# A list scheduler's planned landing times corrected by a table per kind and batch, with a new set of priorities, in a fused attention and MLP kernel

## The chip, the cores and the metric

The kernel runs on one core of one Trainium2 chip. The metric is the device time of one execution in microseconds (us), as the median of three runs. The core has a matrix engine (TensorE, here PE), a vector engine (VectorE, DVE), a scalar engine (ScalarE, ACT), GpSimd (POOL) and SyncE (SP). They run their own instruction streams, each in the order in which it was built, and wait for one another by semaphores. In this kernel POOL issues the loads, and SP issues the transposing transfers and the stores.

## The reference

Masked attention with two kinds of mask, and then a two-layer MLP over all tokens (8 batches of 576 tokens, 8 heads of 64):

```python
B, H, S, D = 8, 8, 576, 64          # x becomes 4608 x 512
scores = scale * (q @ k.transpose)
mask_local = (rel >= 0) & (rel < 32)                       # heads 0 to 3
mask_strided = (rel >= 0) & (pos_k % 32 == pos_q % 32)     # heads 4 to 7
attn = softmax(where(mask, scores, -1e9))
x = (attn @ v)                       # heads side by side, 4608 x 512
h = maximum(x @ w_in, 0)             # 512 -> 2048
out = (s * h * h + b) @ w_out        # 2048 -> 512
```

## The kernel before

**Attention.** The heads of one batch b form four units (b, m): m = 0 and 1 are pairs of local heads, m = 2 and 3 pairs of strided ones. For each unit PE makes the scores (line 840, into the banks ps_s, from kT_loc, kT_alt or a transposed strided key and from the queries spread in qD_loc and qD_str); ACT takes the exponential (858, p_loc, p_str); DVE or POOL apply the mask (866); PE multiplies by the values (901, v_loc, v_str, into ps_a or ps_t); DVE takes the reciprocal of the row sums (918) and multiplies (928, x_nat), which frees the PE bank; x_nat is transposed to xT, by PE (948) or by a DMA (978, and 970 with 974 by way of DRAM). From batch 3 or 4 on, queries and keys are transposed by DMA too: q_dma (788 local, qTl; 796 strided, qT2) and k_dma (768 local, kT_loc and kT_alt; 779 strided, whose place is called vs0 or vs1 after the buffer it reuses, so "vs<-ks" is a key). Copies on DVE or ACT spread qTl and qT2 into qD_loc and qD_str (603).

**MLP.** Tokens go in nine blocks T of 512. The first GEMM (1308, 1549) reads xT and w_in, ACT applies the relu (1330), squares follow (1337, 1339, 1489); the result is gT. The second GEMM (1164, 1276) uses seven products in place of eight (Strassen's scheme) with sums of gT (1043) and of w_out (w_mix, w_sum). A product that completes a quarter of the output is combined on DVE into a tile o (1089), of which there are three, and stored from SP (1111). A fourth combine waits until the first tile's store has landed.

**What sets the order.** All of this is put in order at build time by the class Plan, a list scheduler with a clock of its own. PE's steps are taken one by one; whenever a step is emitted, `flush` places the work of the other engines (a Post) whose needs are met in its clock, the one with the smallest ready time plus priority first. Posts of kind D, X and Y are DMAs of SP: transposes (planned latency 12 us), stores to DRAM and transposes back. `land` gives the planned landing of loads from POOL. The priorities are nine dictionaries ORDER, one for each stretch of the plan's clock (26, 60, 110, 135, 160, 185, 215 and 250 us), with a number for each kind of work ("c11" is the combine of the fourth quarter, "qT" the transposes of queries, "x@V" a bias for x_nat on DVE). The planned times do not run on the chip: they decide only which instruction stands where, and a wrong one makes an engine wait for something behind which other work is queued. `keep_running` lets PE do small filler matmuls (1825, 1830) where the plan has no step.

## Time and profile before

| | |
|---|---|
| median of three runs | 295.19 us (294.97 to 295.9) |
| profiled execution | 295.52 us, its span 293.7 us |
| PE busy | 286.4 us (98%), at the full clock (1.00) |
| DVE / ACT / POOL busy | 232.7 / 207.0 / 97.2 us |
| matmuls | 2873 |

The page's busy times are those of one execution. The chain of waits follows the work that ended last back to its start; a row of a table of waits names the waiting engine and line and, behind the arrow, what ended the wait. In rows of the profile buffer numbers are left out: ps_a stands for ps_a0. Times are counted from the start of the span.

### The profile page before, as it was taken

To read this page: it belongs to the slowest core of one execution; us is meant where nothing else is said; L and a number is where in the kernel's file an instruction comes from. 1 tells how busy PE (TensorE), PEld (TensorE's weight loads), DVE (VectorE), ACT (ScalarE), POOL (GpSimd) and SP (SyncE) were. 2 spreads that over 40 slices of the span, in tenths; PEclk is the share of its full clock that TensorE was granted. 3 is DMA by queue.
4 is the path that set the end of the run, shared out by engine and by line. 5 is a ranking of instruction groups with operands and counts; after the bars stand their busy time and mean duration, and the time that the engine had idled before them with its cause. 6 is when DMAs were issued, how large, how long until landed. Compare 5 with 4: busy or idle time off the path is not lost.

```text
span 293.7 us, 7265 instructions
## 1 busy us (share of the span) xinstructions
PE 286.4 (98%) x2873; PEld 227.2 (77%) x2873; DVE 232.7 (79%) x515; ACT 207.0 (70%) x352; POOL 97.2 (33%) x150
## 2 busy tenths in 40 slices
PE   7999999999999999899999999999999999999995
PEld 3774655666676778799867876799899999999984
DVE  5763887999998699769734998499999877787954
ACT  3559855999998893569789855788756685576700
POOL 8983623610941690339220970540000000000010
PEclk9999999999999999999999999999999999999999
DMA  8999999999999799989997999964212210310214
GB/s 130 193 206 203 214 182 179 192 190 144 132 141 185 80 116 166 138 191 149 202 185 109 128 166 156 161 131 143 57 42 78 71 38 0 109 36 3 72 37 144
DMA packets 95720, 38.18 MB, mean 130 GB/s; under 512 B 73318, under 2 KB 94054, under 8 KB 95686
## 3 DMA queue, kind: packets, MB, share of 16 engines
q0 software_dynamic: 49904, 18.22, 61.3%
q1 hardware_dynamic: 45782, 19.51, 34.6%
q8 instruction: 22, 0.36, 0.5%
q14 instruction: 12, 0.10, 0.1%
HBM read 36.99 MB, written 10.62 MB: 162 GB/s over the span
## 4 chain that ended last, share of the span: by engine, by line
PE 49%; issue 32%; DVE 8%; DMA 4%; POOL 3%; ACT 2%; POOLq 0%; DVEq 0%
PE ps_f L1308 21%; PE ps_f L1164 11%; DMA out_dram<-o 4%; PE ps_s L840 3%; PE ps_f L1580 3%; PE ps_a L901 2%; DVE x_nat L928 1%; PE ps_s L1580 1%; PE ps_t L948 1%; PE ps_f L715 1%; DVE p_loc L866 1%; PE ps_t L715 1%; PE ps_t L901 1%; DVE v_str L603 1%; DVE gT L1339 1%
## 5 line engine op out<-in xcount | busy, mean ns | idle before, releaser
L1308 PE MATMUL ps_f<-xT,w_in_sb 128*128 128x512 f16 (+2 forms) x472 | 100.2, 336 | 0.0
L1330 ACT ACTIVATE gT<-ps_f 128x512 f16<-128x512 f32 x91 | 53.7, 599 | 24.1 <-PE ps_f L1308 19.4
L1164 PEld LDWEIGHTS <-gT 128*128 128x128 f16 x640 | 61.0, 98 | 10.8
L1308 PEld LDWEIGHTS <-w_in_sb 128*128 128x128 f16 x480 | 47.5, 114 | 17.5 <-issue 0.2
L1164 PE MATMUL ps_f<-w_out_sb,gT 128*128 128x256 f16 x400 | 58.2, 273 | 0.0
L1337 ACT ACTIVATE gT<-gT 128x1024 f16<-128x1024 f16 x32 | 33.7, 1062 | 0.7
L1218 POOL TENSOR_TENSOR qD_str<-cp_u,kT_loc 128x512 f32<-128x512 f32 x1 | 1.3, 1262 | 89.3 <-issue 89.3
L1489 ACT ACTIVATE gT<-gT 128x1024 f16<-128x1024 f16 x24 | 25.4, 1058 | 5.3 <-DVE gT L1471 4.2
L1164 PE MATMUL ps_f<-w_mix,gT 128*128 128x256 f16 x208 | 28.9, 273 | 0.0
L1043 DVE TENSOR_TENSOR gT<-gT 128x1024 f16<-128x1024 f16 x40 | 27.2, 698 | 0.2
L928 DVE TENSOR_TENSOR x_nat<-ps_a,rec 96x384 f16<-96x384 f32 (+2 forms) x48 | 24.7, 515 | 0.6
L858 ACT ACTIVATE p_loc<-ps_s 128x384 f16<-128x384 f32 x46 | 20.6, 497 | 3.5 <-PE ps_s L840 3.2
L858 ACT ACTIVATE p_str<-ps_s 72x432 f16<-72x432 f32 (+1 forms) x46 | 20.6, 482 | 2.7 <-PE ps_s L840 2.4
L581 POOL DMA_DIRECT2D v_loc<-in_v_dram x24 | 17.8, 759 | 9.7 <-DMA w_out_sb<-in_moe_w_out_dram 5.9
L1549 PEld LDWEIGHTS <-w_in_sb 128*128 128x128 f16 x176 | 19.3, 114 | 0.5
L901 PEld LDWEIGHTS <-p_str 72*128 72x128 f16 x256 | 13.4, 97 | 5.2 <-issue 1.6
L1164 PE MATMUL ps_f<-w_mix,S 128*128 128x256 f16 x112 | 16.6, 273 | 0.0
L1089 DVE SCALAR_TENSOR_TENSOR o<-ps_f,sb_all,cp_v 128x512 f32<-128x512 f32 x14 | 10.4, 744 | 7.8 <-PE ps_f L1164 5.8
L1043 DVE TENSOR_TENSOR S<-gT 128x1024 f16<-128x1024 f16 x20 | 13.7, 684 | 3.2 <-PE ps_f L1164 3.1
L918 DVE RECIPROCAL rec<-ps_a 96x6 f32<-96x6 f32 (+2 forms) x48 | 8.7, 182 | 9.4 <-PE ps_a L901 9.1
L603 POOL COPY v_str<-v_str 72x512 f16<-72x512 f16 x10 | 6.3, 654 | 28.2 <-DMA v_str<-in_v_dram 28.1
L1580 PE MATMUL ps_f<-w_out_sb,gT 128*128 128x512 f16 x48 | 14.0, 380 | 0.0
(275 smaller groups left out, 589.4 us busy)
## 6 DMA issues: line engine op xcount, KB each, us to landing
out_dram<-o SPq DMA_DIRECT2D x34, 256.0 KB
w_in_sb<-in_moe_w_in_dram POOLq DMA_DIRECT2D x4, 512.0 KB, 9.5
w_out_sb<-in_moe_w_out_dram POOLq DMA_DIRECT2D x4, 512.0 KB, 9.9
qs<-in_q_dram POOLq DMA_DIRECT2D x6, 288.0 KB, 7.9
ks<-in_k_dram POOLq DMA_DIRECT2D x6, 288.0 KB, 9.1
v_loc<-in_v_dram POOLq DMA_DIRECT2D x24, 72.0 KB, 9.8
ql<-in_q_dram POOLq DMA_DIRECT2D x4, 288.0 KB, 9.4
kl<-in_k_dram POOLq DMA_DIRECT2D x16, 72.0 KB, 3.9
```

The source lines that it names most:

```text
L581: nc.gpsimd.dma_start(out=vl[LPAD:128, h, :, 0:D], in_=v_band(b, h))
L858: nc.scalar.activation(out=st["pw", g][0:nk, 0:2 * n * nq], in_=st["s", g][0:nk, 0:2 * n * nq], func=AF.Exp, scale=scale)
L901: nc.tensor.matmul(out=st["pa", g][:, n % 6, :], lhsT=st["pw", gp_][0:nk, i * nq:i * nq + WIDE], rhs=vt[0:nk, 2 * mm + e, j, :])
L928: nc.vector.tensor_tensor(out=x_at(0, cnt), in0=st["pa", g][0:nq, 0:cnt, 0:D], in1=st["rec", g][0:nq, 0:cnt].to_broadcast([nq, cnt, D]), o ...
L1043: {"V": nc.vector, "P": nc.gpsimd}[eng].tensor_tensor(out=at(out), in0=at(x), in1=at(y), op=op)
L1164: nc.tensor.matmul(out=gts[name, T][:, t], lhsT=lhs(k, t), rhs=rhs(k), start=fresh and t == k == 0, stop=t == 1 and k == H - 1, skip_group ...
L1308: nc.tensor.matmul(out=gts["h", T, ft][:, lo:hi], lhsT=w_in_sb[ft // 4][:, ct].rearrange("p (x l) -> p l x", l=4)[:, ft % 4], rhs=xT[ct][: ...
L1330: nc.scalar.activation(out=u, in_=gts["h", T, ft], func=AF.Relu)
L1337: nc.scalar.activation(out=g, in_=g, func=AF.Square)
L1489: nc.scalar.activation(out=g_, in_=g_, func=AF.Square)
L1549: nc.tensor.matmul(out=st[bk][:, 256 * t + lo:256 * t + hi], lhsT=lhs(t, c), rhs=x, start=fresh and t == c == lo == 0, stop=t == c == 1 an ...
L1580: nc.tensor.matmul(out=gts[id_], lhsT=gts[T][:, ft, ts * 128:(ts + 1) * 128], rhs=w_out_sb[:, ft, cols], start=(ft == 0), stop=(ft == NFT ...
```

## The change

A table MORE of 57 numbers (in nanoseconds, between -9000 and +6500) holds corrections of the planned landing times, per kind of load or transfer and batch, and the method `more` looks them up. `land` adds them to loads, `flush` to the transfers of kinds D, X and Y. All nine dictionaries of ORDER have new numbers. No operation, tile or buffer is changed: PE's real matmuls are as many and of the same sizes on every line, and the fillers of line 1830 are 32 in place of 28. Lines behind the table are numbered 36 higher after the change (L1089 is now L1125).

```diff
@@ class Plan
+    @staticmethod
+    def more(k, eng="P"):
+        if k[0] == "in":
+            name, b = k[1], k[2]
+        elif k[0] == "raw":
+            name, b = ("vs", k[3]) if k[1] == "v" else (k[1] + "l" * (len(k[1]) == 1), k[2])
+        elif k[0] in ("k", "qT"):
+            name, b = "T" + k[0][0] + "ls"[k[1][1] // 2], k[1][0]
+        elif k[0] == "xT":
+            name, b = "Txl" if eng == "D" else "Txi", k[1]
+        elif k[0] == "xd":
+            name, b = "Txo", k[1][0]
+        elif k[0] == "soon":
+            name, b = k[0], k[1][0]
+        else:
+            return 0.0
+        return MORE.get(name + str(b), 0.0)
+
     def land(self, keys, cost, late=0.0):
+        late += self.more(keys[0])
...
-                self.done[k] = end + over + ((9000.0 if k[1][0] >= 5 else 6000.0) if soon else p.lat or self.LAT[eng])
+                self.done[k] = end + over + (
+                    (9000.0 if k[1][0] >= 5 else 6000.0) if soon else p.lat or self.LAT[eng]) + (
+                    self.more(k, eng) if eng in "DXY" else 0.0)
...
+MORE = {"Tkl4": 1000.0, "Tkl5": -3500.0, "Tkl7": -1000.0, "Tks3": -5500.0, "Tks4": 1000.0,
+        "Tks5": -6000.0, "Tks6": -9000.0, "Tks7": -9000.0, "Tql6": -6000.0, "Tql7": 2000.0,
...
-    {"SLACK": 1000.0, "ahead": 0.52, "lead": 0.4, "q0": -1500.0, "q": -1160.0, "q@A": -770.0,
...
```

(T stands for a transfer from SP: Tkl the transposes of local keys, Tks of strided ones, Tql and Tqs of queries; the digit is the batch.)

How the rows of the engines move is shown at three places. The first is DVE at 74 to 79 us of the profile, batch 2: the multiplication x_nat, the mask of p_loc and the copies that put values into v_loc1 and v_str1. Before:

```order
L928 TENSOR_TENSOR x_nat_1317<-ps_a0_157,rec_1329 72x384
L603 COPY v_loc1_96<-v_loc1_96 32x2x5x64
L603 COPY v_str1_98<-vs0_105 72x8x64 x4
L603 COPY v_loc1_96<-v_loc1_96 32x2x5x64
L918 RECIPROCAL rec_1380<-ps_a0_157 72x6
L866 TENSOR_TENSOR p_loc0_111<-p_loc0_111,masks_83 128x1152
L928 TENSOR_TENSOR x_nat_1317<-ps_a0_157,rec_1380 72x384
```

After:

```order
L964 TENSOR_TENSOR x_nat_1320<-ps_a0_157,rec_1341 72x384
L902 TENSOR_TENSOR p_loc0_111<-p_loc0_111,masks_83 128x1152
L639 COPY v_loc1_96<-v_loc1_96 32x2x5x64
L954 RECIPROCAL rec_1370<-ps_a0_157 72x6
L639 COPY v_str1_98<-vs0_105 72x8x64 x2
L964 TENSOR_TENSOR x_nat_1320<-ps_a0_157,rec_1370 72x384
L639 COPY v_loc1_96<-v_loc1_96 32x2x5x64
L639 COPY v_str1_98<-vs0_105 72x8x64 x2
```

The second x_nat of the unit stood behind both v_loc copies, all four v_str copies and the mask; it now stands behind the mask, one v_loc copy and two v_str copies, and the other copies follow it.

The second place is DVE at 118 to 123 us, where the second GEMM of block T = 2 begins to give output. o_2038 (before) and o_2044 (after) are the combine that takes over the first o tile of its three, after the store of o_1902 or o_1874; x_nat rows on ps_a0 and ps_t0 free those banks. Before:

```order
L1043 TENSOR_TENSOR gT_1462<-gT_1462 128x4x256 x2
L1089 SCALAR_TENSOR_TENSOR cp_v_115<-ps_f21_161,sb_all_85,bcs_91 128x512
L1043 TENSOR_TENSOR gT_1462<-gT_1462 128x4x256 x2
L918 RECIPROCAL rec_2030<-ps_a0_157 72x4
L1089 SCALAR_TENSOR_TENSOR o_2038<-ps_f20_160,sb_all_85,cp_v_115 128x512
L918 RECIPROCAL rec_2052<-ps_t0_154 72x6
L928 TENSOR_TENSOR x_nat_1896<-ps_a0_157,rec_2030 72x256
L928 TENSOR_TENSOR x_nat_2033<-ps_t0_154,rec_2052 72x384
```

After:

```order
L954 RECIPROCAL rec_2007<-ps_t0_154 72x4
L954 RECIPROCAL rec_2011<-ps_a0_157 72x6
L1125 SCALAR_TENSOR_TENSOR cp_v_115<-ps_f20_160,sb_all_85,bcs_91 128x512
L1079 TENSOR_TENSOR gT_1460<-gT_1460 128x4x256 x2
L964 TENSOR_TENSOR x_nat_2000<-ps_a0_157,rec_2011 72x384
L1125 SCALAR_TENSOR_TENSOR o_2044<-ps_f21_161,sb_all_85,cp_v_115 128x512
L964 TENSOR_TENSOR x_nat_1935<-ps_t0_154,rec_2007 72x256
```

Before, both x_nat (ps_a0, ps_t0) stand behind the combine; after, the one on ps_a0 stands ahead of it and the one on ps_t0 behind. Between o_1902 and o_2038 stood 15 rows with 17 instructions; between o_1874 and o_2044 stand 19 with 20. o_1902 stood behind an x_nat and S (the sum of gT) that follow o_1874 now.

The third place is SP at 102 to 128 us: the stores of block T = 1 (out), the transposes of batch 4's x (xT0, xT1) and those of batch 5's queries (qTl, qT2) and keys (kT_alt, vs0). Before:

```order
L788 DMA_TRANSPOSE qTl_1883<-ql_1712 128x6x96 x2
L1111 DMA out_0_dram<-o_1902 128x2x256
L978 DMA_TRANSPOSE xT0_107<-x_nat_1839 128x6x96
L978 DMA_TRANSPOSE xT1_108<-x_nat_1805 128x6x96
L1111 DMA out_0_dram<-o_1921 128x2x256
L1111 DMA out_0_dram<-o_1950 128x2x256
L768 DMA_TRANSPOSE kT_alt_1958<-kl_1717 128x6x96
L768 DMA_TRANSPOSE kT_alt_1961<-kl_1717 128x6x96
L796 DMA_TRANSPOSE qT2_1988<-qs_769 128x8x80 x2
L779 DMA_TRANSPOSE vs0_105<-ks1_118 128x8x80 x2
```

After:

```order
L1147 DMA out_0_dram<-o_1874 128x2x256
L824 DMA_TRANSPOSE qTl_1892<-ql_1725 128x6x96 x2
L804 DMA_TRANSPOSE kT_alt_1901<-kl_1730 128x6x96
L804 DMA_TRANSPOSE kT_alt_1904<-kl_1730 128x6x96
L1014 DMA_TRANSPOSE xT1_108<-x_nat_1829 128x6x96
L1014 DMA_TRANSPOSE xT0_107<-x_nat_1758 128x6x96
L1147 DMA out_0_dram<-o_1931 128x2x256
L1147 DMA out_0_dram<-o_1973 128x2x256
L832 DMA_TRANSPOSE qT2_1994<-qs_772 128x8x80 x2
L815 DMA_TRANSPOSE vs0_105<-ks1_118 128x8x80 x2
```

The first store passes the two qTl transposes, and the two kT_alt transposes pass xT and two stores; qT2, vs0 and the last store stay where they were. PE's order around this place moves too: from the step of line 901 that waits for the x_nat above (six matmuls on ps_a0 before, four on ps_t0 after) to the first matmul on kT_alt stood 55 matmuls and stand 28; from there to the first on vs0 stood 58 and stand 46.

At the head of the program (17 to 21 us), the last pieces of x_nat of the first batch's two strided units (72x256) move from DVE to ACT, where each is four activations of 72x64, ahead of the copies to xT2 and xT3. On DVE there are 461 rows after and 473 before, on ACT 344 and 331, on POOL 93 and 95, on SP 81 and 77.

## The prediction, made before the run

> **What bounds the kernel now.** I read the busy times of the page first, then the stretches of the span, then what the matrix engine waits for, and last the chain of waits.

> ```profile
> span 293.7 us, 7265 instructions
> PE 286.4 (98%) x2873; PEld 227.2 (77%) x2873; DVE 232.7 (79%) x515; ACT 207.0 (70%) x352; POOL 97.2 (33%) x150
> ...
> 110.00:135.00 25.00, 24.25 (x257) 21.42 (x256) 20.42 (x45) 14.08 (x26) 7.92 (x14) 1.00 1.43 158
> 135.00:160.00 25.00, 25.00 (x226) 19.23 (x225) 15.31 (x33) 22.02 (x34) 8.37 (x13) 1.00 1.37 170
> ```

> The matrix engine, PE, is busy in 286.4 of 293.7 us. In a row of a stretch the first number after its length is PE's busy time, and the two numbers before the last are the granted clock (1.00) and the share of the 16 DMA engines, which is over 1 because packets overlap. From 135 us on PE has no idle time that the profile shows, and its real matmuls are the same in number and size after the change (only fillers differ). So the change can win no more than PE's idle time, and that is listed:

> ```profile
> PE ps_a L901 <- DVE x_nat L928: 1.1, 2, 0.7
> PE ps_s L1825 <- PEq L1928: 0.8, 1, 0.8
> PE ps_t L707 <- DMA ql<-in_q_dram: 0.6, 1, 0.6
> PE ps_f L901 <- POOL v_loc L603: 0.5, 1, 0.5
> PE ps_t L948 <- DVE x_nat L928: 0.4, 1, 0.4
> PE ps_a L707 <- DMA kl<-in_k_dram: 0.2, 1, 0.2
> PE ps_f L840 <- DVE kTs L603: 0.2, 1, 0.2
> PE ps_a L901 <- DVE p_str L866: 0.2, 1, 0.2
> ```

> Each row gives microseconds in all, how often, and the longest. They sum to 4.0 us. The PEq row is the start of the program and the ql, kl, v_loc and kTs rows belong to the first batch (0.6 + 0.2 + 0.5 + 0.2 = 1.5 us), ahead of which the change moves nothing but the size of some fillers: these 2.3 us stay. What can go is x_nat 1.1, x_nat 0.4 and p_str 0.2: **1.7 us**.

> **The head (17 to 42 us).** The 0.4 us is a transposing matmul at 19.1 us that waits for an x_nat. DVE makes three of these in a row there, while ACT waits:

> ```profile
> 18.52 1.31 DVE L928 TENSOR_TENSOR x_nat<-ps_f,rec 72x384 f16<-72x384 f32 x3
> 17.03 0.17 ACT L1639 ACTIVATE sb_all<-ps_f 128x2 f32<-128x2 f32 x1
> 19.69 0.64 ACT L603 COPY xT<-ps_t 128x576 f16<-128x576 f16 x1 [1.83 <-PE ps_t L948]
> ```

> ACT stood 1.83 us ahead of its copy at 19.69 (the bracket). The change gives two narrow pieces of x_nat (72x256) from DVE to ACT, each as four activations of 72x64. DVE is relieved of about 0.4 us each (1.31 for three), so the 0.35 to 0.4 us wait can go. No row has a 72x64 activation; the smallest near it is 0.17 (128x2), so eight take at least 1.4 us, within the 1.83 us that ACT is idle. But they stand ahead of the xT copy, and the second four need a reciprocal that DVE made about 20 us, so that the copy at 19.69 can come some 0.5 us later and the first GEMM with it. I take -0.2, with ends of -0.5 (this and the p_str wait go) and +0.5.

> **The wait at 78.9 us.** The chain of waits (start, duration, what) shows what DVE does in front of it:

> ```profile
> 76.00 1.10 DVE v_str L603 x4
> 77.14 0.41 DVE v_loc L603
> 77.67 0.76 DVE p_loc L866
> 78.42 0.48 DVE x_nat L928
> 78.94 0.28 PE ps_a L901 x4
> ```

> PE stood 0.33 us there (the smaller of the two x_nat waits of ps_a). In the new order the x_nat comes after only two of the four v_str copies and one v_loc copy: 0.55 us and 0.41 us of copies now stand behind it, 0.96 in all, which is more than 0.33. The copies are late by nothing that PE waits for soon, since the values they prepare are read later. I take -0.3; ends -0.4 and 0 (something else on DVE, the reciprocal for example, holds x_nat).

> **The wait at 122.4 us.** This is the longest one, 0.7 us, and its cause lies twelve microseconds back:

> ```profile
> 109.28 0.60 DVE S L1043
> 109.88 0.67 DVE o L1089
> 110.57 10.51 DMA out_dram<-o
> 121.17 0.75 DVE o L1089
> 122.02 0.31 DVE x_nat L928
> 122.38 0.34 PE ps_a L901 x6
> ...
> DVE o L1089 <- DMA out_dram<-o: 2.0, 1, 2.0
> ```

> The last row is from the waits of DVE. There are three o tiles. The fourth combine after 109.88 (o_2038) needs the first one's tile, whose store landed at 121.1; DVE was ready at 121.17 - 2.0 = 119.15 and stood 2.0 us. The x_nat that frees PE's bank stands behind it. PE lost 0.75, so it would have borne some 1.25 us of DVE's wait. Between the two combines DVE worked without a pause from 110.55 to 119.15, 8.6 us for 17 instructions (15 rows), 0.51 us each. In the new order 19 rows with 20 instructions stand between the same two combines: by the mean 1.5 us more, by kinds (two x_nat, a p_str, an S and a reciprocal more, two gT fewer, at some 0.5, 0.7, 0.6, 0.1 and 0.6) about 1.1. The wait shrinks to 0.5 to 0.9 us, below the 1.25 us that PE bears. The next x_nat for ps_a0 even stands ahead of the combine now, but the one for ps_t0, which PE's next step of attention wants first, still stands behind it. So the wait goes if the store takes about as long as before: -0.7, with an end at 0 (the store takes 1 us more, or the waits change banks).

> **What takes its place.** The transposes of batch 5 are issued from SP. First its timeline, then a row of its waits, then two steps of PE in the chain:

> ```profile
> 102.39 3.18 SPq L788 DMA_TRANSPOSE qTl<-ql  x2
> 110.57 0.38 SPq L1111 DMA_DIRECT2D out_dram<-o  x1
> 111.05 4.13 SPq L978 DMA_TRANSPOSE xT<-x_nat  x2
> 115.27 1.07 SPq L1111 DMA_DIRECT2D out_dram<-o  x2
> 116.50 5.62 SPq L768 DMA_TRANSPOSE kT_alt<-kl  x2
> 122.25 3.11 SPq L796 DMA_TRANSPOSE qT<-qs  x2
> 125.90 2.53 SPq L779 DMA_TRANSPOSE vs<-ks  x2
> ...
> SPq L1111 <- DVE o L1089: 4.9, 1, 4.9
> ...
> 127.82 0.33 PE ps_s L840 x4
> 132.90 0.38 PE ps_s L840 x6
> ```

> The store that DVE was late with now stands ahead of the two qTl, which had gone out 8 us before it; kT_alt goes ahead of xT; qT and vs stay last. PE's order wants batch 5 sooner: from the step at 122.38 to the first kT_alt step (127.7) stood 55 matmuls and now 28, and from there to the first step that reads vs (132.7) 58 and now 46. These 39 matmuls at (132.74 - 122.38) / 113 = 0.092 us are 3.6 us: vs is wanted at 129.1, or 128.4 when the wait at 122.4 is gone. When can it be there? The store's combine passes one x_nat and S, 0.49 + 0.60 us, so the store can be issued about 109.5. From there SP's rows add up: 0.4 + 3.2 (qTl) + 5.6 (kT_alt) + 4.1 (xT) + 1.1 (stores) + 3.1 (qT) + 2.5 (vs) = 20.0, to 129.5, against 128.4 before. The first vs, which alone is needed, is through about 1.3 us sooner, 128.2, and must land. PE wants it at 128.4. kT_alt in turn ends near 118.7 and is wanted near 124.2: covered by 5 us. xT moves 4 us later and feeds the stage at 130 and on; the two stores behind it have over 8 us until their tiles come round. So the new wait is between 0 (transposes in an emptier ring take the 1.3 us each that 2.53 for two shows) and +2.0 (the whole 20.0 us and a landing of a microsecond behind it). I take +0.6, nearer to the low end since the SP rows for qTl, qT and vs, 1.3 to 1.6 us each, are more like that than the 2.8 of kT_alt.

> **Everything else.** From 135 us on PE is full, and ACT has 22.02 of 25 us in the first of these stretches, so some small wait may appear: +0.1 (0 to +0.7, the size of the longest now). POOL's queue of loads and copies is two rows shorter; 97 us of work in 293.7 hide that. Fillers are 32 for 28, and run only where PE would stand.

> Sum: -0.2 - 0.3 - 0.7 + 0.6 + 0.1 = **-0.5 us**. The profiled execution took 295.52 us (span 293.7 and 1.8 around it), 0.33 over the median of 295.19. 295.52 - 0.5 = 295.0 for it, and 294.7 as a median. A measurement can tell about 0.3%, 0.9 us, from no change: faster is below 294.3, slower above 296.1.

> **Rivals.** *All stalls go and none comes:* vs is there in time. For it speaks that the first vs is through SP just when PE wants it. -0.5 - 0.4 - 0.75 = -1.65 at best, -1.2 with the taken values: 295.19 - 1.2 to 1.65 gives 293.5 to 294.0, say 293.9. Against it: the DMA share in this stretch is 1.43.

> *The store stays the bound:* the store took 10.51 us at 110.57, but at the end of the program, alone, one takes a quarter of that; and the two kinds of queue were both at work around it:

> ```profile
> 287.96 2.48 DMA out_dram<-o
> ...
> q0 software_dynamic: 8304, 1.77, 78.9%
> q1 hardware_dynamic: 8468, 3.09, 56.5%
> ```

> (the last two rows are the stretch 97 to 132: packets, MB, share). If POOL's loads, which are the same, keep the engines full, the order of SP's rows does not help the store; it has qTl and kT_alt behind it instead of xT. A store of 11.5 us or more takes away term -0.7: -0.2 - 0.3 + 0.6 + 0.1 = +0.2, so 295.4. [...]

> *Slower, batch 5 comes late:* the combine of the store is released by PE and not by DVE's order, so the store goes out at 110.57 as before. qTl then costs its 3.18 on top, vs is through at 128.4 + 3.2 - 1.0 (SP's pauses between its rows) = 130.6 and lands near 131.5, against a wish at 129.1: +2.4, and DVE, with the copies of qTl and qT in its row ahead of masks and x_nat, stands with it. -0.5 + 2.4 + 0.1 = +2.0, or 297.2. It decides from a store issued later than about 110.0. For it: the new place in DVE's row is only 1.1 us earlier. Against it: before, SP stood 4.9 us for DVE's o there, so its rows had time.

> **Chances.** Likeliest (294.2 to 295.1) 0.40; all stalls go 0.27; the store stays the bound 0.15; slower 0.18. Faster: 0.27 and a quarter of the likeliest, 0.37. Slower: 0.18 and a little of the third, 0.19. Same: 0.44. Since both signs hold most, the likeliest one's own range is 294.2 to 295.1; the range that leaves out no more than 2 in 10 runs from the best case, 293.4, to just short of the slow one, 296.9.

> **What would show it.** Right: no wait of PE on x_nat near 79 and 122; the o combine waits under 1.2 us for out_dram; PE's largest new wait is an L876 step (L840 before) on a vs transpose or a qD_str copy near 128. Wrong: a store combine that waits over 2 us, a PE wait over 1 us between 123 and 133, ACT's xT copy after 20.5 us, or waits after 135 us of over 0.7 in sum.

## The result, and the profile after

The changed kernel is slower. Its median is 306.07 us in 6 executions (303.54 to 313.38), against 295.78 us (294.97 to 300.78) for the kernel before on the same chip, a ratio of 1.031 [1.0247, 1.0373]. The prediction was 294.7 us with a range up to 296.9. The profiled execution of the changed kernel took 313.38 us, 2% above its median, so its stalls are read below for their place and order, and what they are worth comes from the comparisons of times.

The page of the changed kernel, its first lines:

```profile
span 311.6 us, 7283 instructions
...
PE 293.2 (94%) x2877; PEld 230.0 (74%) x2877; DVE 227.1 (73%) x506; ACT 217.2 (70%) x370; POOL 99.8 (32%) x147
```

The span is 17.9 us longer. 6.8 us of that are busy time of PE (293.2 against 286.4) for the same real matmuls, of which the slower clock, 0.978 in the mean, would make 6.4 (286.4 / 0.978 - 286.4, an estimate); the rest is waiting. The stretches of the changed kernel (length, busy time of PE, PEld, DVE, ACT, POOL, then the granted clock, the DMA share and GB/s):

```profile
60.00:110.00 50.00, 50.00 (x498) 35.02 (x496) 44.48 (x105) 48.91 (x89) 23.71 (x32) 1.00 1.33 127
110.00:135.00 25.00, 19.13 (x185) 16.20 (x182) 12.99 (x30) 11.90 (x20) 4.83 (x9) 0.93 1.59 133
135.00:160.00 25.00, 23.07 (x227) 19.27 (x228) 14.74 (x36) 19.14 (x33) 12.23 (x18) 0.93 1.44 135
160.00:185.00 25.00, 19.53 (x128) 12.58 (x127) 11.56 (x26) 15.03 (x25) 11.46 (x18) 0.86 1.22 130
```

From 60 to 110 us PE has no gap at all; the loss lies between 110 and 185 us, in three stretches in which the clock is below 1.00 too. What PE waits for in the changed kernel (us in all, times, longest):

```profile
PE ps_f L1200 <- DVE cp_v L1125: 5.5, 1, 5.5
PE ps_s L876 <- DMA kT_alt<-kl: 4.3, 1, 4.3
PE ps_s L876 <- DMA vs<-ks: 3.5, 1, 3.5
...
```

The rows left out are the start of the program (0.8 us) and 0.5 and 0.2 us at the first batch. The waits on x_nat and p_str that the prediction wanted to see go did go, all of them. In their place stand three waits of 3.5 to 5.5 us. Two are for the transposed keys of batch 5; the third, at 170 us, is on DVE, which was itself late. Waits of DVE and of POOL in the changed kernel:

```profile
DVE qD_loc L639 <- DMA qTl<-ql: 12.6, 2, 12.3
DVE qD_str L639 <- DMA qT<-qs: 11.2, 1, 11.2
...
POOL gate L1695 <- DMA vs<-ks: 28.7, 3, 21.9
POOL v_str L639 <- DMA v_str<-in_v_dram: 20.8, 2, 14.6
```

DVE stood 11.2 us for the queries of batch 5 and then 12.3 us for those of batch 6, with its other work in the queue behind. All four waits are for DMAs. The first of them stands on POOL, which issues the loads. Each batch's loads ("fetch") stand behind a copy named gate, which waits for the transposed keys of the batch ahead. POOL in the changed kernel (start, duration, in brackets the time it stood before):

```profile
98.90 1.32 POOL L639 COPY v_str<-v_str 72x512 f16<-72x512 f16 x2 [14.57 <-DMA v_str<-in_v_dram]
...
100.33 2.66 POOL L639 COPY v_str<-v_str 72x512 f16<-72x512 f16 x2
...
103.09 0.69 POOL L1695 COPY gate<-vs 1x1 f16<-1x1 f16 x2
103.75 2.90 POOL L589 DMA_DIRECT2D ql<-in_q_dram  x4
...
137.00 1.39 POOL L1695 COPY gate<-vs 1x1 f16<-1x1 f16 x2 [21.91 <-DMA vs<-ks]
```

The same place in the kernel before:

```profile
91.61 1.16 POOL L603 COPY v_str<-v_str 72x512 f16<-72x512 f16 x2 [7.45 <-DMA v_str<-in_v_dram]
...
98.21 0.18 POOL L1659 COPY gate<-vs 1x1 f16<-1x1 f16 x1 [0.99 <-DMA vs<-ks]
98.73 2.90 POOL L553 DMA_DIRECT2D ql<-in_q_dram  x4 [0.34 <-DVE rec L918]
```

The fetch of batch 5 starts at 103.75 in place of 98.73, 5.0 us later. In the changed kernel both pairs of v_str copies of batch 4 stand on POOL ahead of it (before, one pair, and the other was on ACT), and they waited for a load that took nearly twice as long. The load's rows, KB and us from issue to landing, the batch 4 one and then the batch 5 one, after:

```profile
v_str<-in_v_dram POOLq DMA_DIRECT2D x1, 288.0 KB, 15.3
...
v_str<-in_v_dram POOLq DMA_DIRECT2D x1, 288.0 KB, 17.7
```

and before:

```profile
v_str<-in_v_dram POOLq DMA_DIRECT2D x1, 288.0 KB, 8.2
...
v_str<-in_v_dram POOLq DMA_DIRECT2D x1, 288.0 KB, 13.3
```

From there on everything of batch 5 is late. SP, PE and DVE of the changed kernel:

```profile
107.42 0.38 SPq L1147 DMA_DIRECT2D out_dram<-o  x1
108.32 2.86 SPq L824 DMA_TRANSPOSE qTl<-ql  x2
111.99 6.18 SPq L804 DMA_TRANSPOSE kT_alt<-kl  x2
118.29 6.25 SPq L1014 DMA_TRANSPOSE xT<-x_nat  x2
...
127.02 5.34 SPq L832 DMA_TRANSPOSE qT<-qs  x2
...
126.93 0.49 PE L876 MATMUL ps_s<-qD_loc,kT_alt 128*128 128x192 f16 x4 [4.32 <-DMA kT_alt<-kl]
...
134.41 0.62 DVE L639 COPY qD_str<-qT 64x576 f16<-64x576 f16 x2 [11.21 <-DMA qT<-qs]
...
149.48 16.85 DMA qTl<-ql
```

SP was through with kT_alt at 118.17 and PE could read it at 126.93. The last row is from the chain of waits: the transposes of batch 6's queries, which could not start before the fetch of batch 6 at 138 (before: 131), held the end for 16.85 us.

### The profile page after: what moved, and what is told of

The parts are those of the page before. It is cut to its first block, busy times and chain, and to the rows that moved or that the text cites. A ratio compares the mean times of both kernels' runs of the same rounds, so it can differ in the third digit from the quotient of the medians.

```text
span 311.6 us, 7283 instructions
## 1 busy us (share of the span) xinstructions
PE 293.2 (94%) x2877; PEld 230.0 (74%) x2877; DVE 227.1 (73%) x506; ACT 217.2 (70%) x370; POOL 99.8 (32%) x147
## 4 chain that ended last, share of the span: by engine, by line
PE 79%; DMA 10%; POOL 5%; DVE 2%; issue 2%; SPq 2%; ACT 0%; DVEq 0%; POOLq 0%; ACTq 0%
PE ps_f L1200 22%; PE ps_f L1344 21%; PE ps_f L1585 6%; DMA qTl<-ql 5%; PE ps_s L876 4%; PE ps_f L1616 3%; PE ps_a L937 2%; PE ps_t L1585 2%; DMA qT<-qs 2%; PE ps_s L1200 2%; PE ps_f L1312 2%; PE ps_s L1585 2%; PE ps_a L1585 2%; DMA v_loc<-in_v_dram 1%; PE ps_t L1312 1%
## 5 line engine op out<-in xcount | busy, mean ns | idle before, releaser
L1344 PE MATMUL ps_f<-xT,w_in_sb 128*128 128x512 f16 (+2 forms) x472 | 102.0, 344 | 0.1
L1200 PEld LDWEIGHTS <-gT 128*128 128x128 f16 x640 | 61.5, 99 | 16.6 <-DVE gT L1079 4.1
L1366 ACT ACTIVATE gT<-ps_f 128x512 f16<-128x512 f32 x94 | 55.0, 599 | 26.5 <-PE ps_f L1344 25.3
L1344 PEld LDWEIGHTS <-w_in_sb 128*128 128x128 f16 x480 | 49.1, 115 | 20.5 <-issue 1.7
L1200 PE MATMUL ps_f<-w_out_sb,gT 128*128 128x256 f16 x400 | 57.5, 275 | 0.0
L1373 ACT ACTIVATE gT<-gT 128x1024 f16<-128x1024 f16 x37 | 39.2, 1059 | 0.7
L1200 PE MATMUL ps_f<-w_mix,gT 128*128 128x256 f16 x208 | 30.4, 279 | 5.5 <-DVE cp_v L1125 5.5
L1525 ACT ACTIVATE gT<-gT 128x1024 f16<-128x1024 f16 x24 | 25.2, 1056 | 7.3 <-DVE gT L1507 6.8
L617 POOL DMA_DIRECT2D v_loc<-in_v_dram x24 | 17.7, 748 | 9.0 <-DMA v_loc<-in_v_dram 3.2
L1585 PEld LDWEIGHTS <-w_in_sb 128*128 128x128 f16 x176 | 19.2, 114 | 0.7 <-issue 0.2
L937 PEld LDWEIGHTS <-p_str 72*128 72x128 f16 x256 | 12.6, 97 | 3.9 <-DVE p_str L902 0.2
L639 POOL COPY v_str<-v_str 72x512 f16<-72x512 f16 x8 | 7.3, 943 | 20.9 <-DMA v_str<-in_v_dram 20.8
L1200 PEld LDWEIGHTS <-S 128*128 128x128 f16 x128 | 12.7, 100 | 1.8
```

The source lines that it names most:

```text
L617: nc.gpsimd.dma_start(out=vl[LPAD:128, h, :, 0:D], in_=v_band(b, h))
L937: nc.tensor.matmul(out=st["pa", g][:, n % 6, :], lhsT=st["pw", gp_][0:nk, i * nq:i * nq + WIDE], rhs=vt[0:nk, 2 * mm + e, j, :])
L1200: nc.tensor.matmul(out=gts[name, T][:, t], lhsT=lhs(k, t), rhs=rhs(k), start=fresh and t == k == 0, stop=t == 1 and k == H - 1, skip_group ...
L1344: nc.tensor.matmul(out=gts["h", T, ft][:, lo:hi], lhsT=w_in_sb[ft // 4][:, ct].rearrange("p (x l) -> p l x", l=4)[:, ft % 4], rhs=xT[ct][: ...
L1366: nc.scalar.activation(out=u, in_=gts["h", T, ft], func=AF.Relu)
L1373: nc.scalar.activation(out=g, in_=g, func=AF.Square)
```

## The experiments

The theories at the start: (1) the priorities alone cost the time, (2) the table's entries for loads or for transfers cost it, by making the planner put work in an order that the real landings do not keep; and within (2), either POOL's v_str copies ahead of the fetch, or SP's transposes of batch 4 among the loads of batch 4, or SP's order around batch 5 (the prediction's slower rival). The first eight kernels were built to separate these.

**The priorities without the table.**

```diff
-MORE = {"Tkl4": 1000.0, ...}
+MORE = {}
```

> The new priorities with an empty table of corrections. Theory A (the table made the planner count on batch 4's strided V some 4.5 us sooner and so put two copies that wait for it ahead of POOL's fetch of batch 5; the loads of batch 5 then start at 103.8 us in place of 98.7): without the table the copies are planned later and the fetch of batch 5 is issued before 101 us; time 296 to 300. Rival B (the priorities themselves set an order in which the transfers collide, with or without the table): 302 to 308, waits of PE over 3 us between 115 and 170 us again.

297.53 us (297.33 to 297.78), ratio 1.0082 [1.0066, 1.0098]. No wait of PE over 0.8 us is left, and the fetch of batch 5 is at 98.06. So the new priorities alone cost some 2.4 us, and the other three quarters need the table. In this profile PE is busy 287.9 us against 286.4 before (1.1 us of it in fillers) and idle 8.1 against 7.3, so no single wait has the 2.4 us. The time and the fetch came out as Theory A forecast, but its mechanism did not: both pairs of v_str copies of batch 4 stand on POOL ahead of the fetch without the table too. They cost nothing there, since V had landed by 91.8:

```profile
91.77 1.16 POOL L629 COPY v_str<-v_str 72x512 f16<-72x512 f16 x2 [9.60 <-DMA v_str<-in_v_dram]
...
93.04 1.27 POOL L629 COPY v_str<-v_str 72x512 f16<-72x512 f16 x2
...
98.06 2.88 POOL L579 DMA_DIRECT2D ql<-in_q_dram  x4 [0.34 <-DVE x_nat L954]
```

What the table adds is therefore not the place of these copies but that the load which they wait for lands late.

**The table with the old priorities**: the nine dictionaries of the kernel before, MORE as in the change.

> The old priorities with the table. Theory A (the corrections hold only for the order in which they were measured): slower than before, 297 to 304, with a transfer wanted by PE sooner than it lands at one or two places between 100 and 180 us. Rival (the corrections are right and only the new priorities lose): 294 to 296.5, and no wait of PE over 1 us behind the head.

312.75 us (305.76 to 316.2), too scattered for a ratio. Its profile shows other stalls than the changed kernel's (4.2 us on a p_str mask, 1.9 on a gT), and its fetch of batch 5 is in time, at 98.25. All four executions are above 305 us, so the table is harmful with the old priorities too, though not by the same stall and not by a late fetch. V of batch 5 took 16.4 us to land.

**Transfers alone, loads alone.** The table was split: only the entries whose name begins with T, then only the others.

> New priorities, and of the table only the entries for SP's transfers (names that begin with T). Theory D (the harm comes from the entries for loads: they make the planner count on batch 4's loads 4.5 to 6 us sooner, which sends the transposes of batch 4 among the loads that are still under way): 296 to 299, like the priorities alone (297.5). Rival E (the harm comes from the entries for transposes, which make PE want the keys of batch 5 sooner): 301 to 307 with waits of PE on kT_alt or vs over 2 us.

> New priorities, and of the table only the entries for loads. Theory D: 301 to 307, with the load of batch 4's strided V over 12 us from issue to landing, the fetch of batch 5 after 102 us, and waits of PE on kT_alt or vs of some 4 us each. Rival E: 296 to 299.

Transfers alone: 297.39 us, 1.0068 [1.0048, 1.0088], fetch at 97.53, the same as without a table. Loads alone: 305.65 us (302.09 to 308.36), too scattered for a ratio, with the fetch at 102.76 and waits of 2.0 us on kT_alt and 1.6 on kT_loc, less than the 4 us each that were expected. Without the entries for loads the table adds nothing to what the priorities cost; with them alone the time is near that of the whole change.

**The copies behind the fetch.** A post that is held is placed as planned, but its instructions are issued only behind another post:

```diff
+            if p.keys[0] in HOLD:
+                self.held.setdefault(HOLD[p.keys[0]], []).append((p, eng))
+            else:
+                p.fn(eng)
+HOLD = {("in", "vs", 4, 0): ("fetch", 5), ("in", "vs", 4, 1): ("fetch", 5)}
```

> The changed kernel, with one edit: the two v_str copies of batch 4 on POOL are issued behind the fetch of batch 5's queries and keys instead of ahead of it; all other engines keep their order. Theory A: the first load of batch 5 is issued at 99 to 101 us in place of 103.8, the waits of PE on kT_alt and vs between 120 and 140 (7.8 us in the changed kernel's profile) shrink to under 3, time 297 to 301. Rival B (SP's order of batch 4's transposes slows the loads) and rival C (SP's order of store, qTl and kT_alt is at fault): 302 to 307, the waits stay.

300.23 us, 1.0214 [1.0146, 1.0281]. The fetch moved to 101.71 only, since the gate then waited for vs, and PE had a new wait, for the copies:

```profile
PE ps_t L948 <- POOL v_str L692: 2.6, 1, 2.6
```

The kT_alt step had no wait there (125.18). The edit moves one thing more: the copies now stand between batch 5's loads of queries and keys and those of its V, whose strided load goes out 14.5 us behind the start of the fetch (116.19) in place of 10.4, and lands in 9.6 us in place of 17.7.

**SP's order at batch 4 as before**: the transposes of batch 4's keys leave the loads of their own batch alone.

```diff
+HOLD = {("k", (4, 0)): ("xT", 3, 0), ("k", (4, 1)): ("xT", 3, 0), ("k", (4, 2)): ("qT", (4, 3))}
```

> The changed kernel, with one edit: SP issues batch 4's transposes in the order of before (xT, then the two kT_loc; qT2 before both vs). Rival B: the load of batch 4's strided V lands in 8 to 10 us as before (15.3 in the changed kernel's profile), so that POOL's copies and the fetch behind them come at about 98 us; time 296 to 300. Theory A without B (that load is late for another reason): it still takes over 12 us, the fetch stays near 103.5, time 302 to 307.

301.13 us, 1.019 [1.0162, 1.0217], between the two forecasts. V of batch 4 landed in 10.4 us in place of 15.3, and the fetch was at 100.29. But V of batch 5 still took 16.6 us and kT_alt was late:

```profile
PE ps_s L888 <- DMA kT_alt<-kl: 4.0, 1, 4.0
PE ps_s L888 <- DMA vs<-ks: 1.6, 1, 1.6
```

**Both edits together.**

> The changed kernel with both edits of the former runs: POOL's two v_str copies of batch 4 behind the fetch of batch 5, and SP's transposes of batch 4 in the order of before. Each alone gave back 4 to 5 us of about 10. If they are two causes that add (late fetch, slow load): 296 to 298. If they are one chain (both only bring the fetch forward): 298.5 to 301, no better than the better of the two.

297.08 us in 10 executions, 1.0065 [1.0035, 1.0094].

```profile
100.10 2.90 POOL L603 DMA_DIRECT2D ql<-in_q_dram  x4 [0.37 <-DVE v_loc L653]
...
PE ps_s L890 <- DMA vs<-ks: 0.9, 1, 0.9
```

Five held posts, three on SP and two on POOL, with the table and the priorities as they are, take the ratio from 1.031 to 1.0065, four fifths of the loss, and leave what the priorities alone cost. V of batch 5 lands in 9.1 us. This shows the place: the loads and transposes of batches 4 and 5. It does not show that the late fetch is what costs: with SP's edit alone the fetch was at 100.29 and the time 301.13, with both edits at 100.10 and 297.08. As in the kernel with the copies alone, the held copies also send the strided V load later behind the fetch (113.79, 13.7 us, in place of 10.4). No kernel tells these two effects apart.

**SP's order around batch 5 as before**, the prediction's own cause for a slower kernel: kT_alt held behind the combine ("c10", 1), and the store of block 1 sent behind the two qTl transposes.

> The changed kernel, with one edit: SP issues around batch 5 in the order of before (both qTl ahead of the store, the two kT_alt behind xT and the two stores). The prediction's slower rival (the store ahead of qTl makes batch 5 late): 297 to 301. Theory A (the fetch of batch 5 is late on POOL, whatever SP's order): 303 to 309, since kT_alt is issued still later and is waited for longer.

304.94 us, 1.0313 [1.0234, 1.0393], no better than the change. The store went out at 107.42 in the changed kernel, sooner than before, and moving it back gives

```profile
PE ps_s L887 <- DMA kT_alt<-kl: 7.2, 1, 7.2
```

so giving SP its order of before at batch 5 takes nothing off.

**Which loads of the table.** Three kernels left out the entries for loads of batch 4 (kl4, ks4, ql4, qs4, vl4, vs4), of batch 5 (kl5, ks5, qs5, vl5, vs5), and of both.

> New priorities, the table without its six entries for the loads of batch 4 (kl4, ks4, ql4, qs4, vl4, vs4). If these six send the transposes and copies of batch 4 among its loads and so start the chain: 296 to 299, fetch of batch 5 before 100.5 us. If the entries for later batches do the harm as much: 300 to 306.

> New priorities, the table without its five entries for the loads of batch 5 (kl5, ks5, qs5, vl5, vs5); those of batch 4 stay. Without batch 4's the time was 305.5, so those did not do it alone. If batch 5's entries are the ones that matter (they bring the transposes kT_alt and PE's wish for them forward): 296 to 299.5. If either group is enough by itself: 301 to 306.

> New priorities, the table without the entries for loads of batches 4 and 5. If the harm is done by these eleven: 296 to 299.5, like the priorities alone and the transfers alone (297.5 and 297.4). If entries for batches 3, 6 and 7 or the sum of all do it: 301 to 306.

305.46 us (1.0352 [1.0332, 1.0372]), 307.31 (1.0399 [1.034, 1.0459]) and 304.79 (1.0312 [1.0267, 1.0356]). None recovers anything. Without batch 4's entries (the first and the last) V of batch 4 lands in 9.8 and 9.7 us, as quickly as with the priorities alone (10.3); with them, and without batch 5's, it takes 13.8. So in these profiles, one of each kernel, the six entries bring the late landing of V, and yet the time stays without them: V of batch 5 takes 15.1, 20.3 and 16.9 us. The fetch stands at 100.74, 102.58 and 100.45, and each has its own stall: 4.3 us on a p_str mask and 2.4 on kT_alt, 9.5 on kT_alt, 8.5 on kT_alt in two. I had expected one group to carry the loss; it does not. Entries of batches 3, 6 and 7 are left in all three, and which entries matter is not settled.

**Is a late fetch enough by itself?** The kernel before, with idle copies on POOL ahead of the fetch of batch 5 and nothing else changed:

```diff
+        if b == 5:
+            for _ in range(n):          # n = 24, then 10
+                nc.gpsimd.tensor_copy(out=idle, in_=idle)
         load_qk(b)
```

> The kernel before, with one edit: some 5 us of copies on POOL ahead of the fetch of batch 5's queries and keys, so that its loads start at about 103.5 in place of 98.7; nothing else moves. Theory A (a late fetch alone makes the waits of PE on batch 5): 299 to 305, with a wait of PE on kT_alt, qTl or vs near 127 to 133 of 3 us or more. Rival (the order before has the slack for it, and the late fetch costs only with PE's earlier wish for batch 5): 295 to 297.

> The kernel before with the fetch of batch 5 held back on POOL by some 5 us (the former such kernel held it back by 11.7 us, which cost 12). Theory (the order before has no more than 1 to 2 us to spare for batch 5's data, and beyond that each microsecond of lateness is a microsecond of PE's wait, with the clock's fall on top when a wait passes 4 us): 298 to 301. Rival (a late fetch is mostly absorbed, and 11.7 us is past the point where it is not): 295 to 297.

With 24 copies the fetch came at 110.28, 11.6 us late where 5 had been meant, and the time was 307.02 us, 1.038 [1.0358, 1.0403]. With 10 it came at 102.48, 3.8 us late: 298.05 us, 1.0111 [1.0076, 1.0146]. In this order a late fetch costs 0.8 to 1.0 us for each microsecond: 12.1 for 11.6, 3.1 for 3.8. The 10-copy kernel has the changed kernel's wait, on the same tile:

```profile
PE ps_s L840 <- DMA kT_alt<-kl: 0.9, 1, 0.9
```

So the kernel before has little to spare for that fetch. By this price the changed kernel's 5.0 us would be 4 to 5 of the 10.3 us between the medians, and the priorities 2.4 more; that is an estimate, since the price was measured in another order. It does not carry over to the other kernels with the table: with SP's order of before at batch 4 the fetch was 1.6 us late and the loss 1.9%, some 5.6 us; without the entries of batches 4 and 5 it was 1.7 us late and the loss 3.1%, some 9 us; with the table and the old priorities it was in time.

What goes with the times better is how long the strided V load of batch 5 takes. In the six kernels without inserted stalls in whose profile it landed in 8.5 to 9.9 us the time is 295.0 to 300.2 us. In the eleven in whose profile it took 14.8 to 20.3 us the time is 301 us and more, with one exception (the 10-copy kernel, 15.7 us and 298.05). The profile of the kernel before lies between, at 13.3 us. The two are only seen together, which is no experiment: the load can be slow for the same reason as the transposes beside it.

**Late data or an early wish?** The changed order also wants batch 5 sooner. Two kernels take the two apart. In the changed one, PE's first step of each unit of batch 5 was kept back until 127.5 us of the plan's clock:

```diff
+            if p // 4 == 5 and at_i[p] == 0 and plan.t < 127500.0:
+                continue
```

> The changed kernel, whose orders on SP and POOL stay as they are up to 130 us; only PE's first steps on batch 5's keys (kT_alt) are put 42 matmuls later in its row, about 4.5 us, and what follows is planned anew. Theory F (the loss comes from PE asking for batch 5's keys 4 to 5 us sooner while they land at about 127 in all these kernels): the wait on kT_alt is under 1 us, time 297 to 301. Rival G (the loss comes from late data: the fetch at 103.8 and what hangs on it): the data come as late as before, other work of batch 5 and 6 waits instead, 302 to 307.

In the kernel before, the method `more` with a table of one entry made PE want it sooner:

```diff
+MORE = {"Tkl5": -4000.0}
```

> The kernel before with a table of one entry (the transposes of batch 5's local keys planned 4 us sooner); loads, SP and POOL keep their order up to there, PE's first steps on kT_alt stand 28 matmuls earlier, about 2.6 us. Theory F: PE waits 1.5 to 3 us on kT_alt near 126, 296.5 to 300. Rival G: no such wait, 294.7 to 296.

The late wish: 306.17 us, 1.0349 [1.0319, 1.0379]. The kT_alt step ran without a wait, and PE stood later for ACT, which itself had stood 9.32 us for the strided queries of the same batch (DVE stood 11.22 us for them):

```profile
127.10 0.49 PE L876 MATMUL ps_s<-qD_loc,kT_alt 128*128 128x192 f16 x4
...
135.54 1.86 PE L1344 MATMUL ps_f<-xT,w_in_sb 128*128 128x192 f16 x8 [7.62 <-ACT gT L1366]
...
133.51 1.36 ACT L639 COPY qD_str<-qT 64x576 f16<-64x576 f16 x2 [9.32 <-DMA qT<-qs]
```

The early wish: 295.61 us, 1.0021 [0.9992, 1.005]. Its kT_alt step ran at 123.55, as early as the prediction had it for the changed kernel, and without a wait, since the fetch was at 98.69 and SP was done with the transposes at 119.5:

```profile
98.69 2.89 POOL L576 DMA_DIRECT2D ql<-in_q_dram  x4 [0.34 <-DVE rec L941]
...
115.87 3.66 SPq L791 DMA_TRANSPOSE kT_alt<-kl  x2
...
123.55 0.49 PE L863 MATMUL ps_s<-qD_loc,kT_alt 128*128 128x192 f16 x4
```

A late wish saves nothing and an early one costs nothing while the data come in time: the data are late; the wish is not too early.

**What the removed waits were worth.** The kernel before, with two of the change's moves done by hand: the v_str and v_loc copies behind the x_nat at 78.9, and the o combine of block 2 behind an x_nat at 122.

```diff
+HOLD = {("in", "vs", 3, 1): ("x", (2, 3), 1), ("in", "vl", 3, 0): ("x", (2, 3), 1),
+        ("c00", 2): ("x", (4, 3), 0)}
```

> The kernel before, with DVE's order changed at the two places of the prediction only: two v_str copies and a v_loc copy of batch 3 behind the x_nat that PE waits for at 78.9, and the combine that waits for a store behind the two x_nat at 122. By the prediction's terms, -0.3 and -0.7: 294.0 to 294.4, and no wait of PE on x_nat at either place. Rival (the waits move to the next thing that DVE is late with): 294.8 to 295.5.

295.01 us in 11 executions, 1.0006 [0.9994, 1.0019]. The two waits are absent from its profile and the time is unchanged, as the rival forecast.

**Stalls and the clock.** The kernel before, with three stalls of PE late in the program: a matmul on a tile idle, n POOL copies of that tile, and a matmul that needs them. First long ones, then short ones.

> The kernel before, with three stalls of PE on copies of POOL put in, near 222, 238 and 254 us, of about 2, 3 and 5 us (it computes the same). If the granted clock is halved for some microseconds after a stall of more than about 3.5 us and not after shorter ones: 1.00 after the first two, 0.50 for 3 to 6 us after the third, and the time 295 plus the three stalls plus 2 to 3. If the clock falls for another reason (the state of the run, not the stall): 1.00 throughout, 295 plus the three stalls.

> The kernel before, with three stalls of PE on POOL's copies of about 2.4, 2.8 and 3.2 us (it computes the same). Stalls of 4.05, 6.2 and 8.65 us were each followed by 3.4 us and more at a clock of 0.50, and in other profiles one of 3.5 us was and one of 4.0 us was not. [...] If shorter stalls halve it too: 0.50 after each, and 5 us more.

320.52 us with stalls of 4.05, 6.22 and 8.65 us (18.9 in sum), 310.73 with 2.64, 3.39 and 2.99 (9.0 in sum), one execution each, against 294.94. That is 25.6 and 15.8 us, so 6.7 and 6.8 more than the stalls themselves: some 2.2 for each stall in both, though the long ones are twice as long. In the profile of the short ones, microsecond by microsecond around the first (the stall ends at 224.13):

```profile
223.00:224.00 1.00, 0.00 (x0) 0.00 (x0) 0.00 (x0) 0.00 (x0) 0.82 (x4) 0.91 0.00 0
224.00:225.00 1.00, 0.87 (x5) 0.64 (x6) 0.00 (x0) 0.00 (x0) 0.08 (x1) 0.50 0.00 0
...
227.00:228.00 1.00, 1.00 (x10) 0.88 (x9) 0.93 (x3) 0.00 (x0) 0.00 (x0) 0.88 0.42 147
228.00:229.00 1.00, 1.00 (x12) 0.97 (x10) 0.97 (x5) 0.51 (x2) 0.00 (x0) 1.00 0.33 115
```

The granted clock is 0.50 until 227, and then 1.00 again. The kernel with the long stalls also answers another question. Its order is the kernel before's up to 222 us, and its DVE hardly waited for the store of which the prediction made its largest term:

```profile
119.95 0.75 DVE L1089 SCALAR_TENSOR_TENSOR o<-ps_f,sb_all,cp_v 128x512 f32<-128x512 f32 x1 [0.16 <-DMA out_dram<-o]
```

0.16 us in this execution, 2.0 in the one profiled before. In the kernel with the short stalls, whose order up to there is the same, DVE did not wait for a store there at all, and in neither does PE wait on x_nat near 122.

No version beats the kernel before: the nearest are the hand-made swaps (1.0006) and the early wish (1.0021).

## Why the prediction was wrong

**The bound, and what could be won.** PE's idle time was the right measure for the gain: 1.7 us at most. It is no bound for a loss, and the prediction weighed the loss at one place alone. The step that failed is the sum for that place, the transposes of batch 5 (+0.6, with ends 0 and +2.0). It took the durations and the landings of loads and transposes as one profile of the other order had them; in their place PE stood 4.3 and 3.5 us for batch 5's keys, 5.5 us more at 170, and ran at a clock of 0.50 for 3.4, 3.4 and 6.8 us about their ends.

**Head, 78.9 and 122.4 (-0.2, -0.3, -0.7).** The mechanisms were right: all waits on x_nat and p_str are gone after the change, and from 60 to 110 us PE is busy in 50.00 of 50.00 us. The sizes of the last two were wrong. Done by hand, both together gave a ratio of 1.0006 [0.9994, 1.0019], nothing, where -1.0 us was booked (0.9966). For the term at 122.4 the reason is shown: the 2.0 us of DVE and PE's 0.7 belonged to one execution, in which the store was slow, and in two others with the same order DVE stood 0.16 us and not at all. For the -0.3 no reason was looked for; PE's 0.3 us wait itself recurs in those two executions. The head was not tried by itself; ACT's copy that could come some 0.5 us later came at 20.05 in place of 19.69.

**The new wait (+0.6, ends 0 and +2.0).** The place and the sign were right: PE's new waits are L876 steps on batch 5's keys. The sum of SP's rows behind it failed in two terms. First, "kT_alt in turn ends near 118.7 and is wanted near 124.2: covered by 5 us" takes the end of SP's issue for the landing. SP was through at 118.17, close to the forecast, and the step ran at 126.93, 8.8 us later. With a fetch in time the cover of 5 us does exist: in the kernel with the early wish 4.0 us (119.5 to 123.55) were enough. Second, the sum took SP's durations from the kernel before, 1.3 to 1.6 us for each transpose of a query or vs. After the change two transposes of qT took 5.34 in place of 3.11, and two of xT 6.25 in place of 4.13, in a stretch (110 to 135 us) whose DMA share rose from 1.43 to 1.59.

**"POOL's queue of loads and copies is two rows shorter; 97 us of work in 293.7 hide that."** This put a term at nothing for the wrong reason. A share of busy time says nothing about a queue that is in order: the fetch of batch 5 stood behind copies that waited 14.57 us for V of batch 4, and came 5.0 us late. The kernel before with a fetch 3.8 us late lost 1.1%, with one 11.6 us late 3.8%. The order on POOL could have been read ahead of the run, as that of DVE and SP was. It would have shown what the fetch can wait for and not that it would: with the priorities alone the same copies stand ahead of it and it is in time. The late landing of V of batch 4 could not be read from the order.

**"From 135 us on PE is full ... +0.1."** There the profiled execution lost 5.47 us at 170, and the clock besides. There the wait was not for ACT, which the prediction named, but for DVE, and the chain of that execution leads back over DVE's 12.25 us for the queries of batch 6 and their transposes to the fetch of batch 6, at 138 in place of 131, behind the gate that waits for batch 5's keys.

**The rivals.** "Slower, batch 5 comes late" was right in sign and in what is late, and wrong in cause and size. Its condition, a store issued after 110.0, was not met (107.42), and SP's order of before around batch 5 gave 1.0313. Its +2.0 us held one wait and neither batch 6 nor the clock. "The store stays the bound" was wrong about the store. What it feared for SP's rows beside POOL's loads is seen on a load: V of batch 4 took 8.2 us to land before, 15.3 after, and 10.4 with SP's transposes of batch 4 moved out of its way. "That all stalls go" failed at the same place.

**What is shown and what is not.** Shown: three quarters of the loss need the table's entries for loads; five held posts at batch 4 give back four fifths; a late fetch alone costs 0.8 to 1.0 us for each microsecond in the order of before; the data are late and not the wish early; the copies stand ahead of the fetch by the priorities, and in the profiles taken V of batch 4 lands late with batch 4's entries for loads and in time without them. Argued only: that the late fetch is what costs the changed kernel its time. Against it speak the kernels with a fetch less than 2 us late, or in time, that lose as much. The rival, that loads and transposes of batch 5 meet on the DMA engines whenever the fetch starts, was not tried by itself; the edits that helped also moved the V load away from the transposes. Open too: which single entries matter, and where the 2.4 us of the priorities alone go.

## What to carry to other kernels

Corrections of landing times that change the order can change the landings themselves: here the load of V of batch 4 landed after 15.3 us in place of 8.2. When a change moves instructions, read first the queue that issues the loads and ask what stands ahead of each fetch and what that waits for, whatever the busy share of its engine (POOL's was 32%); whether it will wait depends on landings that an order does not show. A stall of one microsecond seen in one profiled execution is not yet a term of a sum: look for it in a second execution of the same order first.

## What the runs showed of the hardware

```profile
124.00:126.00 2.00, 0.00 (x0) 0.00 (x0) 0.00 (x0) 0.00 (x0) 0.00 (x0) 1.00 1.49 105
...
128.00:130.00 2.00, 2.00 (x12) 1.33 (x10) 0.00 (x0) 0.76 (x2) 0.00 (x0) 0.50 1.38 87
130.00:132.00 2.00, 2.00 (x16) 1.64 (x15) 0.00 (x0) 0.97 (x3) 0.00 (x0) 0.71 1.32 126
```

Over the profiled execution it is 0.978 in the mean; in the executions near the median it is 0.988 to 0.989, which by 286.4 / 0.9885 - 286.4 would be 3.3 of the 10.3 us, an estimate. In the two kernels with idle stalls the clock fell to 0.50 at all six, of 2.64 to 8.65 us, within the stall or up to 1.02 us behind it. At a stall of 3.96 us in the kernel with SP's batch 4 order it did not:

```profile
123.00:127.00 4.00, 0.23 (x3) 0.00 (x0) 0.61 (x2) 1.16 (x2) 0.00 (x0) 1.00 1.22 57
127.00:131.00 4.00, 3.81 (x38) 3.49 (x39) 0.47 (x2) 2.84 (x6) 0.00 (x0) 1.00 1.17 292
```

nor did it at the one of 2.6 us with the copies behind the fetch (1.00 from 108 to 148 us), so the length alone does not decide.

The clock stood at 0.50 from 127.73 to 131.14, 137.97 to 141.38 and 168.69 to 175.51 us in the changed kernel, that is for 3.41, 3.41 and 6.82 us. With the long stalls it was 226.42 to 229.83, 246.90 to 253.73 and 270.79 to about 281.0: 3.41, 6.83 and 10.2 us. With the short ones it was 223.82 to 227.24, 244.30 to 251.12 and 268.20 to 271.60: 3.4, 6.8 and 3.4 us. A time inside a row is worked out from the row's mean clock, with 1.00 on one side and 0.50 on the other. The fall came now before the end of a stall and now behind it: 2.33 us into the short stall of 2.64 us, and 0.80 us after PE was at work again behind the 4.32 us. What sets the moment of the fall and of the return is not shown.

**The load of V and the transposes beside it.** The strided V load of batch 4, 288 KB from POOL, took 12.5 to 15.3 us from issue to landing in the four kernels with the whole change and its order of SP at batch 4 (the changed one, the copies behind the fetch, SP's order at batch 5, the late wish). It took 10.4 and 10.1 us in the two in which SP's transposes of batch 4 stand as before. For batch 5 the same load took 17.7 us after the change, and 13.3 in the profiled execution of the kernel before. That execution was not typical: in three other kernels that keep its order of loads up to there (the early wish, the long stalls, the two swaps) it took 9.4, 9.8 and 9.9 us. From 98 to 118 us the DMA engines of the changed kernel moved 115 GB/s, its two queues q0 and q1 at a share of 75.7 and 54.3%; with the five held posts it was 125 GB/s, at 91.8 and 34.2%. Why is open. The pair of kT_alt transposes, from SP, took 2.61 to 4.10 us of SP's time in the six kernels without inserted stalls where that V load of batch 5 took under 10 us, and 3.72 to 8.38 where it took 14.8 us or more, so in these profiles the two are often slow together, though they are issued by different engines. I had booked a transfer's time as its own.
